# Row matrices of the lead-in sort split over POOL, ScalarE and VectorE

## The chip, the cores and the metric

The kernel runs on one core of one Trainium2 chip. The metric is the device time of one execution in microseconds (us). For the kernel before, three runs gave 8667.58, 8670.53 and 8680.19 us; the median is 8670.53 us.

## What is computed

A graph has N = 10000 nodes and E = 640000 edges. Every edge takes the 64 x 4 features of its source node, multiplies them with a 4 x 4 matrix made of the edge's Y and the tensor cg, scales each channel with a radial weight, and adds the result to its target node. At the end the 64 channels are mixed:

```python
R = _silu(edge_feat @ w_rad)                              # (E, C)
xs = x[src]                                               # (E, C, M)
tp = jnp.einsum('eci,ef,ifo->eco', xs, Y, cg)             # (E, C, M)
msg = R[:, :, None] * tp
agg = _segment_sum(msg.reshape(-1, C * M), dst, N).reshape(N, C, M)
return jnp.einsum('ncm,cd->ndm', agg, w_mix)
```

## The kernel before

The segment sum needs the edges of a target node together, so the kernel sorts the edges' payloads (9 words: a key of target and source, four of Y, four of edge_feat) by target in two passes. The first pass (`pass1`) sorts into 18 groups of 576 nodes, the second (`pass2`) each group into buckets of 32 nodes; `messages` then gathers the source rows and does the arithmetic bucket by bucket. The edges are cut into three parts (`SPLIT`, 30%, 35.5%, 34.5%). Pass 1 of the first part runs alone at the start: this is the **lead-in**, 1488 tiles of 128 edges. Everything later (pass 1 of the other parts, pass 2, the messages) is interleaved by `groups`, which starts when the lead-in's groups lie in DRAM: its first load, `Wt` (L760), reads what the lead-in has stored.

A pass takes its tiles in chunks, twelve tiles each in pass 1, so the lead-in has 124 chunks (0 to 123). `route` moves a chunk with one matmul per tile: the payloads, spread over 14 slots of a row (`spread`: the mask L569 and `X` L572, VectorE), are multiplied by a 128 x 128 matrix that is one where the row of the edge equals the column. These **row matrices** `oh` come from `rows`. Of a chunk's twelve, VectorE makes the first six with one comparison (L588; its constant 0..127, `v128`, is in PSUM), and ScalarE the last six with a Square each (L594: (row - i)^2) and one Relu of 1 - 2x over all six (L595). TensorE accumulates the twelve products in PSUM (L602; each float32 product is two MATMUL records in the trace), ScalarE copies the result to `rt` (L609), and POOL stores its 128 rows to the DRAM tensor `grp` with one indirect DMA (L613). The positions come from small matmuls (L532, L534), ScalarE (L542) and VectorE (L551 to L561), the payload words from L714 to L716, and every 20 chunks or so a table is worked out (`digits`, `tables`).

`oh` and `X` have three buffers each, `rt` has 38 in the lead-in.

What sets the order. In the lead-in the order on SP is the order in which the code issues; for the other engines a planner lays down one list per engine beforehand, from its own estimates of when each instruction can start, earlier code first where several can. On the chip each engine goes through its list. In the code a chunk's store comes eight chunks behind its row matrices (`self.ls`). SP's list holds the loads of the edges (`ys`, `es`, `da`, `si`) and, woven between them, the zeroing of what later stages write: first the buckets (`bkt<-z`, L248), then the groups of parts 1 and 2 (`grp<-z`, L230, 36 DMAs of about half a MB). The latter go to the tensor `grp`, which the indirect stores of the lead-in also may write anywhere, so a clear waits for the stores that precede it in the code, and the stores that follow wait for the clear. In the list planned for the kernel before, the store of chunk 102, the first one behind the last clear, stands behind the row matrices of chunk 108.

In the rest of the kernel PE, VectorE and ScalarE follow an order written out by `groups`.

Of the kernel before, what the change touches and what calls it, by code (L numbers as in the profile page):

```python
# [21 lines left out]
OP = mybir.AluOpType  # L22
# [3 lines left out]
P = 128  # L26
# [30 lines left out]
def weave(main, side, ratio):  # L57

    acc = 0.0
    for said in main:  # L60
        acc += ratio
        while acc >= 1.0:
            acc -= 1.0
            next(side, None)
        yield said
    yield from side


def run(gen):
    for _ in gen:  # L70
        pass


class Kernel:
# [276 lines left out]
    def tables(self, ps, D, nt, rows, kov, base, cap):  # L351
# [157 lines left out]
        self.tab[ps.key] = (sb, idx, N, tg if ps.carry else None)  # L509
        yield  # L510

    def route(self, ps, quad, nt, table):


# [2 lines left out]
        nc, wk, tc, T, Q = self.nc, self.ph, self.tc, ps.T, 2  # L517
# [60 lines left out]
        def rows(c):  # L578

            row, _ = MS[c // (2 * Q)]  # L580
            o = c % (2 * Q) * T
            m = min(T, nt - c * T)
            (_, _, _, tg), i = table(c)
            on = ps.carry and i > 0
            oh = self.ph.tile([P, 12, P], F, name="oh", bufs=3)
            v = max(m - ps.act, 0)
            if v:
                nc.vector.tensor_tensor(oh[:, :v, :], self.v128.unsqueeze(1).to_broadcast([P, v, P]),  # L588
                                        row[:, o:o + v].unsqueeze(2).to_broadcast([P, v, P]), op=OP.is_equal)

            at = [row[:, o + u:o + u + 1] for u in range(v, m)] + ([tg[:, i - 1:i]] if on else [])
            sq = self.ph.tile([P, 7, P], F, name="sq")
            for u, to in enumerate(at):
                nc.scalar.activation(sq[:, u, :], self.i128, AF.Square, bias=to, scale=-1.0)  # L594
            nc.scalar.activation(oh[:, v:v + len(at), :], sq[:, :len(at), :], AF.Relu, bias=self.ones[:, 0:1], scale=-2.0)  # L595
            XO[c] = (XO[c], oh, m, on)
# [26 lines left out]
        for k in range(-3 * Q, N + self.ls):  # L623
            if 0 <= k - lag - 1 < N:
                evict(k - lag - 1)
            if 0 <= k - lag < N:
                move(k - lag)
            if k % 2 and 0 <= k + 5 < N:

                while self.pos:  # L630
                    yield "held"
                self.pos = ps.key
                places((k + 5) // 2)
            if k % 2 == 0 and 0 <= k + 4 < N:
                placed((k + 4) // 2)
                self.pos = None
            if k % 2 == 0 and 0 <= k + 6 < N:
                prepare((k + 6) // 2)
            if 0 <= k < N:
                spread(k)  # L640
                yield "half"
                rows(k)
            if k % 2 and 0 <= k + 3 < N:
                slots((k + 3) // 2)
            if 0 <= k - self.ls < N:
                store(k - self.ls)

            yield (HEAVY - 2 if k < N else HEAVY) if 0 <= k < N + lag else 1

    def pass1(self, part, first):  # L650
# [73 lines left out]
        while True:  # L724

            if side is None and j + 1 < nb and (j < 1 or k >= cut[j]):
                j += 1
                side = front(j)
            need = of[min(max(k + 6, 0), nch - 1)] not in TB
            if side is not None and (need or acc >= 1.0 or self.held == ps.key):  # L730
                acc -= 1.0
                said = next(side, "end")
                if said == "end":
                    side = None
                    continue
                yield said
                if need or said != "held":
                    continue
                acc = 0.0
            said = next(route, "end")  # L740
            if said == "end":
                break
            if said == "half":
                yield 2
                continue
            if said != "held":
                k = k + 1
                acc = min(acc + 2.0, 8.0)
            yield said
# [289 lines left out]
    def groups(self):  # L1039
# [26 lines left out]
        for v in range(4 * u):  # L1066
# [24 lines left out]
            next(main)  # L1091
        assert not later
        run(main)
        run(sort)

    def chunks(self, part):
# [109 lines left out]
    def run(self):  # L1206
        tile_pool, nc = self.tc.tile_pool, self.nc
        order = [self.NG - 1] + list(range(self.NG - 1))
        self.segs = [(k, g) for k in range(len(SPLIT)) for g in order]
        with tile_pool(name="p1", bufs=2) as self.ph:  # L1210
            self.rt_bufs, self.ls = 38, 8
            self.lag, self.ahead, self.early = 2, 3, 1
            self.z = self.ph.tile([P, 2048], F, name="z", bufs=1)
            nc.gpsimd.memset(self.z, 0.0)
            self.consts()

            with self.tc.manual_schedule(engines={mybir.EngineType.SP}):
                first = self.pass1(0, 8)
                next(first)
                run(self.clear_groups(0, nc.scalar))  # L1220
                for _ in range(40):
                    next(first, None)
                while self.held:
                    next(first)
                self.weights()
                later = itertools.chain(self.clear_buckets(),
                                        *(self.clear_groups(k, nc.sync) for k in range(1, len(SPLIT))))
                run(weave(first, later, 0.185))
                self.sorted = 1
        with tile_pool(name="p2", bufs=2) as self.ph:  # L1230
            self.rt_bufs, self.ls = 5, 4
            self.lag, self.ahead, self.early = 1, 2, 0
            self.p1.NC = 14
            with self.tc.manual_schedule(engines={mybir.EngineType.PE, mybir.EngineType.DVE,
                                                  mybir.EngineType.Activation}):
                self.groups()
        with tile_pool(name="p3", bufs=1) as self.ph:
            self.overflow_consts()
            self.overflow(self.p1, self.kov[:, 0:1])
            self.overflow(self.p2, self.kov[:, 1:2])  # L1240
# [29 lines left out]
```

## Time and profile before

| | us |
|---|---|
| median of 3 runs | 8670.53 |
| time of the profiled execution, as its span | 8660.7 |
| what the median has beyond that span | 9.8 |
| last store of the lead-in starts (L613) | 523.22 |
| first load of the next stage issues (L760) | 525.91 |

Times inside a profile count from the start of its span. A row of the timeline gives start, duration, engine, line, operation and tiles, how many were merged, and in brackets the engine's idle time before it with what seems to have ended it. A row of the windows view gives, for a stretch, its length and then for each engine the busy time and in parentheses the number of instructions; the last three columns are TensorE's granted clock, the busy share of the DMA engines and the GB/s. The lines view gives busy time, mean ns of one instruction, and the idle time before. "SPq" is the issue of a DMA on SP's queue.

### The profile page before, as it was taken

What the parts mean: (1) busy time and instruction counts of PE and PEld (TensorE: products, weight loads), DVE (VectorE), ACT (ScalarE), POOL (GpSimd) and SP (SyncE); (2) the same over time, 40 slices, a digit from 0 to 9 for tenths busy, and PEclk for the clock granted to TensorE, in tenths of its full rate; (3) what the DMA queues carried; (4) which work ended last, traced back from release to release, by engine and by line L of the source; (5) the groups of instructions that cost most, each with busy time, mean ns of one, the idle gap of its engine ahead of it and who ended that gap; (6) DMA issues with size and microseconds to landing.
All of it is one profiled execution on the core that took longest, in us unless ns stands there. A gap on an engine that the chain in (4) does not pass through costs nothing. (4 is left out here: it accounts for less than half of the span.)

```text
span 8660.7 us, 149335 instructions
## 1 busy us (share of the span) xinstructions
PE 6942.9 (80%) x52148; PEld 6380.0 (74%) x52148; DVE 7173.7 (83%) x13741; ACT 4089.0 (47%) x11736; POOL 6041.3 (70%) x6308
## 2 busy tenths in 40 slices
PE   7978888888888778888888888866888878788875
PEld 6867777777777677777777777766777767777764
DVE  8989899889998788999989998877877768677754
ACT  6866555555556455454544554433333323333310
POOL 1236777667777767777777777777777777777775
PEclk9989999889999889999889899888998889888887
DMA  9313434334433434444444444444444444444442
GB/s 169 104 58 99 123 115 119 103 113 117 121 110 111 122 106 132 135 132 138 133 130 136 135 133 134 128 138 132 128 125 125 125 124 124 122 128 125 124 123 83
DMA packets 696289, 1056.64 MB, mean 122 GB/s; under 512 B 252018, under 2 KB 500226, under 8 KB 695536
## 3 DMA queue, kind: packets, MB, share of 16 engines
q0 software_dynamic: 286560, 746.71, 30.3%
q1 hardware_dynamic: 406384, 292.76, 12.2%
q8 instruction: 412, 6.75, 0.3%
q10 hardware_dynamic: 2592, 7.63, 0.3%
q14 instruction: 341, 2.79, 0.1%
HBM read 856.08 MB, written 207.12 MB: 123 GB/s over the span
## 5 line engine op out<-in xcount | busy, mean ns | idle before, releaser
L893 POOL DMA_INDIRECT xg<-in_x_dram,sidx x5321 | 5067.8, 952 | 1739.3 <-issue 1386.5
L602 PE MATMUL pr<-X,oh 128*128 128x126 f32 (+1 forms) x21112 | 2765.2, 289 | 395.7 <-ACT rt L609 215.6
L958 PE MATMUL G<-S,xg 128*128 128x128 f32 x21284 | 2953.1, 302 | 98.1 <-DVE Gp L987 62.8
L602 PEld LDWEIGHTS pr<-X,oh 128*128 128x128 f32 x21112 | 2638.2, 201 | 477.8 <-ACT rt L609 264.2
L958 PEld LDWEIGHTS G<-S,xg 128*128 128x128 f32 x21284 | 2803.5, 215 | 139.3 <-DVE Gp L987 86.2
L945 DVE TENSOR_TENSOR xg<-xg,pre 128x1536 f32<-128x1536 f32 (+1 forms) x939 | 1556.8, 1658 | 710.5 <-DMA xg<-in_x_dram,sidx 586.4
L594 ACT ACTIVATE sq<-i,rowf 128x128 f32<-128x128 f32 x5605 | 1735.7, 393 | 13.9 <-DVE rowf L559 13.4
L572 DVE TENSOR_TENSOR X<-dv,Wt 128x1512 f32<-128x1512 f32 (+4 forms) x958 | 1588.4, 1658 | 149.0 <-PE pr L602 94.8
L927 ACT ACTIVATE pre<-pre 128x384 f32<-128x384 f32 (+1 forms) x939 | 430.8, 459 | 1694.7 <-PE pre L924 1204.7
L595 ACT ACTIVATE oh<-sq,ones 128x768 f32<-128x768 f32 (+3 forms) x958 | 932.1, 973 | 32.9 <-issue 5.5
L938 DVE TENSOR_TENSOR S<-dv,pay 128x768 f32<-128x768 f32 (+1 forms) x939 | 857.4, 913 | 48.0 <-PE G L958 2.8
L613 POOL DMA_INDIRECT grp<-rt,idx x417 | 415.5, 996 | 585.9 <-ACT rt L609 240.1
L588 DVE TENSOR_TENSOR oh<-dv,rowf 128x640 f32<-128x640 f32 (+2 forms) x922 | 792.2, 864 | 0.5
L613 POOL DMA_INDIRECT bkt<-rt,idx x541 | 543.2, 1004 | 221.7 <-issue 125.8
L911 PE MATMUL pre<-identb,e 128*108 128x128 bf16 x1878 | 277.3, 231 | 523.4 <-DVE xg L945 513.6
L911 PEld LDWEIGHTS <-e 128*108 128x108 bf16 x1878 | 219.9, 133 | 604.5 <-issue 515.2
L916 ACT ACTIVATE sT<-pre 108x256 bf16<-108x256 f32 x939 | 353.5, 376 | 631.1 <-PE pre L911 628.4
L1006 PE MATMUL po<-wf,Gs 128*128 128x256 f32 (+2 forms) x1392 | 382.3, 436 | 150.7 <-DVE Gs L987 150.5
L542 ACT ACTIVATE pc<-pp 128x432 f32<-128x432 f32 (+3 forms) x506 | 243.7, 482 | 524.1 <-DVE pos L551 407.3
L1006 PEld LDWEIGHTS po<-wf,Gs 128*128 128x128 f32 (+2 forms) x1392 | 277.5, 205 | 238.3 <-DVE Gs L987 166.8
L609 ACT ACTIVATE rt<-pr 128x135 f32<-128x135 f32 (+1 forms) x958 | 258.8, 273 | 269.4 <-DMA bkt<-rt,idx 181.4
L923 PE MATMUL pre<-wr,sT 108*128 108x192 bf16 x939 | 240.2, 256 | 142.2 <-ACT sT L916 141.8
(240 smaller groups left out, 5309.3 us busy)
## 6 DMA issues: line engine op xcount, KB each, us to landing
xg<-in_x_dram,sidx POOLq DMA_INDIRECT x5321
sums<-Gp SPq DMA_DIRECT2D x626, 128.0 KB
old<-sums SPq DMA_DIRECT2D x626, 128.0 KB
bkt<-z SPq DMA_DIRECT2D x24, 994.5 KB
pay<-bkt SPq DMA_DIRECT2D x34, 486.0 KB
ys<-in_Y_dram SPq DMA_DIRECT2D x104, 96.0 KB
es<-in_edge_feat_dram SPq DMA_DIRECT2D x104, 96.0 KB
out_dram<-ot SPq DMA_DIRECT2D x69, 128.0 KB
```

Source lines behind the costliest of these rows:

```text
L572: nc.vector.tensor_tensor(X[:, :m, :].rearrange("p t (s w) -> p t s w", w=W), msk.unsqueeze(3).to_broadcast([P, m, ps.r, W]), QD[c // Q][1 ...
L588: nc.vector.tensor_tensor(oh[:, :v, :], self.v128.unsqueeze(1).to_broadcast([P, v, P]), row[:, o:o + v].unsqueeze(2).to_broadcast([P, v, P ...
L594: nc.scalar.activation(sq[:, u, :], self.i128, AF.Square, bias=to, scale=-1.0)
L595: nc.scalar.activation(oh[:, v:v + len(at), :], sq[:, :len(at), :], AF.Relu, bias=self.ones[:, 0:1], scale=-2.0)
L602: nc.tensor.matmul(pr[:, :ps.rw], oh[:, u, :], X[:, u, :], start=(u == 0), stop=(not on and u == m - 1))
L613: st = nc.gpsimd.indirect_dma_start(out=ps.dst, out_offset=bass.IndirectOffsetOnAxis(ap=idx[:, i:i + 1], axis=0), in_=RT.pop(c), in_offset ...
L893: nc.gpsimd.indirect_dma_start(out=xg[:, t, :], out_offset=None, in_=self.x, in_offset=bass.IndirectOffsetOnAxis(ap=si[:, u:u + 1], axis=0))
L911: nc.tensor.matmul(pre[:KR, 256 + 128 * h:384 + 128 * h], e[:, 36 * t:36 * t + KR], self.identb, start=True, stop=True)
L938: nc.vector.tensor_tensor(S[:, :ut], self.eq[:, :ut].unsqueeze(3).to_broadcast([P, ut, NB, 4]), pb[:, :, 1:5].unsqueeze(2).to_broadcast([P ...
L945: nc.vector.tensor_tensor(V, V, R.unsqueeze(3).to_broadcast([P, ut, 64, 4]), op=OP.mult)
L958: nc.tensor.matmul(G[:, h].rearrange("p n f -> p (n f)"), V[:, t, 32 * h:32 * h + 32, :].rearrange("p c i -> p (c i)"), S[:, t].rearrange( ...
L1006: nc.tensor.matmul(po[:nn, :256], Gs[:, h, f].rearrange("p b n -> p (b n)")[:, :nn], self.wf[:, h, f, :], start=(h + f == 0), stop=(h + f ...
```

## The change

In the lead-in the comparison for the first five tiles of a chunk moves to POOL, one `tensor_scalar` per tile, against the same constant in SBUF (`i128`) with the tile's row numbers as a per-partition scalar. VectorE keeps two tiles (the sixth and seventh), ScalarE the last five. `self.aid` is 5 in the lead-in and 0 in the rest, where the split stays as it was.

```diff
+    def act(self, ps):
+        return 5 if self.aid else ps.act
...
-            v = max(m - ps.act, 0)
-            if v:
-                nc.vector.tensor_tensor(oh[:, :v, :], self.v128.unsqueeze(1).to_broadcast([P, v, P]),
-                                        row[:, o:o + v].unsqueeze(2).to_broadcast([P, v, P]), op=OP.is_equal)
+            v = max(m - self.act(ps), 0)
+            g = min(self.aid, v)
+            for u in range(g):
+                nc.gpsimd.tensor_scalar(oh[:, u, :], self.i128, row[:, o + u:o + u + 1], None, op0=OP.is_equal)
+            if g < v:
+                nc.vector.tensor_tensor(oh[:, g:v, :], self.v128.unsqueeze(1).to_broadcast([P, v - g, P]),
+                                        row[:, o + g:o + v].unsqueeze(2).to_broadcast([P, v - g, P]), op=OP.is_equal)
...
             self.lag, self.ahead, self.early = 2, 3, 1
+            self.aid = 5
...
             self.lag, self.ahead, self.early = 1, 2, 0
+            self.aid = 0
```

## The prediction

> **What bounds the kernel now.** The change touches only the lead-in, so the first question is where the lead-in ends and what ends it. I read the windows view first (columns PE, PEld, DVE, ACT, POOL, then clock, DMA share, GB/s), in the stretches that the rest of the argument uses.
>
> ```profile
> span 8660.7 us, 149335 instructions
> 40.00:240.00 200.00, 168.57 (x1256) 148.05 (x1255) 176.50 (x367) 151.07 (x457) 37.46 (x38) 0.92 0.92 154
> 240.00:496.00 256.00, 239.36 (x1900) 212.51 (x1900) 251.83 (x465) 229.09 (x691) 62.37 (x64) 0.99 0.28 95
> 496.00:521.00 25.00, 23.63 (x195) 22.16 (x194) 20.92 (x23) 16.06 (x46) 18.81 (x20) 1.00 0.15 45
> ```
>
> From 240 to 496 us VectorE is busy 251.83 of 256 us, TensorE 239.36, ScalarE 229.09, POOL 62.37. Seen like this, moving work from VectorE to the idle POOL looks free. The timeline says otherwise. These are POOL's and SP's rows at four places, and the first of the next stage:
>
> ```profile
> 214.25 0.97 POOL L613 DMA_INDIRECT grp<-rt,idx  x1 [1.77 <-ACT rt L609]
> 240.32 0.97 POOL L613 DMA_INDIRECT grp<-rt,idx  x1 [25.09 <-ACT pc L542]
> ...
> 288.12 0.97 POOL L613 DMA_INDIRECT grp<-rt,idx  x1 [0.30 <-ACT Wt L715]
> 290.45 0.34 SPq L230 DMA_DIRECT2D grp<-z  x1
> 295.07 0.97 POOL L613 DMA_INDIRECT grp<-rt,idx  x1 [5.98 <-ACT Wt L715]
> 296.35 0.97 POOL L613 DMA_INDIRECT grp<-rt,idx  x1 [0.30 <-ACT sq L594]
> ...
> 496.41 0.97 POOL L613 DMA_INDIRECT grp<-rt,idx  x1 [4.30 <-ACT oh L595]
> ...
> 523.22 0.97 POOL L613 DMA_INDIRECT grp<-rt,idx  x1 [0.30 <-issue]
> 525.91 0.34 SPq L760 DMA_DIRECT2D Wt<-grp  x1
> 526.02 0.18 DVE L770 TENSOR_SCALAR base<-bb 128x18 f32<-128x18 f32 x1 [8.17 <-DMA grp<-rt,idx]
> ```
>
> The next stage starts when the last store has landed (525.91, and VectorE has then idled 8.17 us). From 240 us on the stores do not follow the compute; they alternate with the clears of `grp` on SP: a store (288.12) lands, the next clear issues (290.45), it lands, and the next stores go (295.07, 296.35). POOL stands idle some 6 us for each clear, and the brackets name engines that have nothing to do with it. How many clears, stores and row matrices there are:
>
> ```profile
> L230 SPq DMA_DIRECT2D grp<-z x36: 332/343/1655, 234.0 to 493.4; - x36
> L613 POOL DMA_INDIRECT grp<-rt,idx x124: 969/971/1315, 44.1 to 523.2; - x124
> 0.00:240.00 240.00, 37.46 (x38) 0.94 0.90 168
> 240.00:496.00 256.00, 62.37 (x64) 0.99 0.28 95
> 496.00:525.00 29.00, 21.39 (x22) 0.98 0.15 46
> 0.00:240.00 240.00, 43.47 (x46) 0.94 0.90 168
> 240.00:496.00 256.00, 66.80 (x71) 0.99 0.28 95
> ```
>
> The third to fifth rows are the windows of L613, the last two those of L588. Between 240 and 496 us 36 clears and 64 stores make 256 us, or 7.1 us a clear and 4.0 us a store. Meanwhile 71 chunks got their row matrices, one per 3.6 us. So the stores fall behind: the 38 + 64 = 102 stores done at 496 us stand against 46 + 71 = 117 chunks whose VectorE half has begun, a lead of 15. The 22 stores that are left then go in one run, 1.275 us apart (26.81 us from 496.41 to 523.22), and only just catch up with the last chunk. **Two limits meet at 524 us**: the compute, and the chain of clears and stores. Relief for VectorE shifts only the first.
>
> **The change, part by part.** Rows for the durations:
>
> ```profile
> L572 DVE TENSOR_TENSOR X<-dv,Wt 128x1512 f32<-128x1512 f32 x73 | 126.0, 1727 | 1.9
> L588 DVE TENSOR_TENSOR oh<-dv,rowf 128x768 f32<-128x768 f32 x72 | 68.1, 945 | 0.0
> L588 DVE TENSOR_TENSOR oh<-dv,rowf x922: 275/818/958, 37.8 to 8265.1; 128x640 f32<-128x640 f32 x100, 128x768 f32<-128x768 f32 x82, 128x128 f32<-128x128 f32 x3
> L594 ACT ACTIVATE sq<-i,rowf 128x128 f32<-128x128 f32 x434 | 135.8, 398 | 2.8 <-DVE rowf L559 2.5
> 499.55 2.92 PE L602 MATMUL pr<-X,oh 128*128 128x126 f32 x24 [0.16 <-DVE oh L588]
> 502.62 2.91 PE L602 MATMUL pr<-X,oh 128*128 128x126 f32 x24 [0.16 <-DVE oh L588]
> L149 POOL IOTA i<- 128x128 f32 x1 | 0.2, 236 | 0.0
> L267 POOL IOTA prm<- 128x128 f32 x1 | 0.4, 438 | 0.0
> L1214 POOL MEMSET z<- 128x2048 f32 x1 | 1.8, 1804 | 0.3 <-POOLq L1258 0.3
> ```
>
> *VectorE.* Six tiles take 945 ns, one takes 275, so a tile is (945 - 275) / 5 = 134 ns and two tiles 0.41 us: 0.54 us less per chunk. *ScalarE* loses one Square of six, 135.8 / 434 = 0.31 us of its time, and a sixth of a Relu. Neither of the two can shorten a chunk much below the present pace: undisturbed, a chunk takes 502.62 - 499.55 = 3.07 us, and TensorE's own 24 records take 2.91 of it. Even without any other limit the pace gains 0.16 us of 3.07, or 5%.
>
> *Up to 240 us.* The DMA engines are 92% busy here, TensorE 168.57 of 200 us. VectorE idles 23.5 us and would lose 40 x 0.54 = 22 us of work, so the bounds of an earlier first clear are 0 and 22 us. I take **-5 us**, near the lower end, as SP's list reaches that clear only behind the bucket zeroing, and that is DMA time.
>
> *POOL's new work.* No POOL comparison is in this trace. The nearest rows of the same 128 x 128 size are the two iotas, 0.236 and 0.438 us, which only write; the memset makes 0.88 ns an element, 0.11 us for 128. One `tensor_scalar` also reads, so I take 0.30 us, with 0.20 and 0.44 as ends: **1.5 us per chunk** (1.0 to 2.2). By itself that fits beside a store of 1.275 us: 2.8 us of a chunk's 3.6.
>
> *What is queued behind a blocked store.* The five comparisons of a later chunk now stand in POOL's list between stores. A store that waits for a clear holds up every comparison behind it, then the matmuls of that chunk, and with three `oh` buffers soon VectorE and ScalarE. The free lead of 15 chunks is gone; what is left is the lead of the planned list, where store 102 stands behind the row matrices of chunk 108. I assume that the new list keeps about that, with one chunk more as POOL is otherwise free. Then at the last clear 14 chunks' comparisons are still to be made, where the trace has 7 left. POOL must from 496.41 on do 22 stores and 14 groups of five: 22 x 1.275 + 14 x 1.5 = 49.1 us, so the last store ends at 545.5 instead of 524.2: **+21 us** (TensorE needs 14 x 2.91 = 41 us beside it, which does not decide). With 1.0 and 2.2 us a group it is +14 and +31 us.
>
> [...]
>
> *The chain between 240 and 496 us.* 63 groups of comparisons (45 to 108) must run in it, 94 us by my price. POOL's idle time there is 256 - 62.37 = 194 us, so they can lie under the waits for clears. Those that the list puts between a clear's landing and the next stores lengthen that round instead. Ends: none, and all 94 us. POOL is in its run of stores about a quarter of the time (62.37 of 256 us), so I take a fifth: **+19 us**.
>
> [...]
>
> *The sum:* -5 + 21 + 19 = +35 us. Everything behind L760 runs as before, with `self.aid` 0 and its order written out, so the shift goes through to the end: span 8660.7 + 35 = 8695.7, and with the 9.8 us that the median has beyond the span, **8705.5 us**. The cover on which the change lives is POOL's idle time; it is idle because it waits, and that is the time in which it can't do anything else either.
>
> **The rivals.** About 0.2% (17 us) is what a measurement of this kernel can tell from no change.
>
> *The comparisons get past the stores* (the new list runs them far ahead, or POOL is not held). For it: the planner knows of the clears, and a faster compute in its estimate would widen the lead. Against it: three `oh` buffers. Then compute gains up to 5%, but the 36 clears at 7.1 us and 22 stores end where they did, less what the first clear comes earlier: 0 to -22 us, 8648 to 8670.5. Most of that lies within 17 us, since the DMA engines hold the first clear.
>
> *POOL becomes the bound.* At 0.44 us a comparison, a chunk's store and group take 1.275 + 2.2 = 3.5 us, as long as a chunk now. If besides every group falls into a round of the chain, the price is 63 x 2.2 + 31 = 170 us, 8840 us. It decides from about 0.35 us a comparison, or where the list puts the comparisons behind the landing. Half of that, +85 us, is where I part it from the forecast.
>
> *The split doesn't reach the clock at all*: list and lead stay and the tail is hidden: 8670 us, part of "same".
>
> **How the numbers follow.** Forecast (+17 to +85 us): 0.60. POOL as the bound (above +85): 0.15. No coupling, within 17 us: 0.16. No coupling and an early first clear, below -17: 0.09. So slower 0.75, within 0.2% 0.16, faster 0.09. The range goes from -10 us (8660), inside the case without coupling, to +100 us (8770), a little into POOL as the bound; about 0.1 lies beyond each end.
>
> **What would show it.** Right: the new profile has POOL rows of L588's place between the stores, of some 0.3 us each; waits of TensorE for POOL's `oh` from 240 us on; a lead of some 8 chunks instead of 15 where the last clear lands; the last store near 545 to 560 us and L760 behind it by 2.7 us; the rest of the span as long as before. Wrong: clears that still issue 7.1 us apart with compute running ahead of the stores as before (then the coupling fails), a last store before 520 us, a comparison far from 0.3 us, or a change behind L760.

## The result and the profile after

The changed kernel takes 8732.41 us (median of 5 runs, 8727.85 to 8734.75) against 8675.29 us for the kernel before beside it: a ratio of 1.0067, 95% interval 1.0056 to 1.0078, or 57 us slower. Forecast were 35 us, with a range that reaches to 100. The profiled execution has a span of 8730.1 us, 69.4 more than before. That is more than the 57 us because the profiled execution of the kernel before (span 8660.7 us) was quicker than all five of its runs here (8667.58 us and more), while the changed kernel's median lies 2.3 us beyond its span. The runs were taken in batches, each with the kernel before beside it, and in one batch everything behind the lead-in took longer (10586.37 us for the kernel before), so that of this batch only ratios and lead-in ends count.

The same four places of POOL's and SP's timeline, in the changed kernel (the store is now L619, the comparison L592, the next stage's load L766). First the stores around 245 us, where the clears of `grp` begin, then the first store behind the last clear, then the **run-out** (the 22 stores behind the last clear) and its end:

```profile
245.56 1.25 POOL L619 DMA_INDIRECT grp<-rt,idx  x1 [0.17 <-issue]
247.11 0.97 POOL L619 DMA_INDIRECT grp<-rt,idx  x1 [0.30 <-PE pp L537]
248.11 2.94 POOL L592 TENSOR_SCALAR oh<-i,rowf 128x128 f32<-128x128 f32 x5
255.06 1.05 POOL L619 DMA_INDIRECT grp<-rt,idx  x1 [4.02 <-PE pp L537]
...
533.88 1.05 POOL L619 DMA_INDIRECT grp<-rt,idx  x1 [0.17 <-issue]
...
550.98 2.93 POOL L592 TENSOR_SCALAR oh<-i,rowf 128x128 f32<-128x128 f32 x5
554.09 1.05 POOL L619 DMA_INDIRECT grp<-rt,idx  x1 [0.17 <-ACT sq L600]
555.19 2.93 POOL L592 TENSOR_SCALAR oh<-i,rowf 128x128 f32<-128x128 f32 x5
...
595.82 0.97 POOL L619 DMA_INDIRECT grp<-rt,idx  x1 [0.30 <-issue]
598.55 0.34 SPq L766 DMA_DIRECT2D Wt<-grp  x1
```

Five comparisons take 2.93 us, 0.59 us each, where 0.30 was put in. Towards the end POOL does nothing but five comparisons and one store, over and over, 4.2 us a chunk (550.98 to 555.19), without a pause. Split at the same stores as before, the lead-in became longer like this:

| | before | after | difference |
|---|---|---|---|
| store 38 starts | 240.32 | 245.56 | +5.2 |
| store 38 to store 102 (the chain with the clears) | 256.1 | 288.3 | +32.2 |
| store 102 to store 123 (the run-out) | 26.8 | 61.9 | +35.1 |
| last store to the next stage's load | 2.7 | 2.7 | 0.0 |
| everything behind that load, to the end of the span | 8134.8 | 8131.6 | -3.2 |

The whole loss is in the lead-in, as forecast; 72.6 us there, and what follows is as long as it was. How the loss splits between the chain and the run-out depends on the profile of the kernel before that one compares with (last experiment); their sum changes by 7 us. The windows of the changed kernel (columns PE, PEld, DVE, ACT, POOL, clock, DMA share, GB/s):

```profile
40.00:240.00 200.00, 174.99 (x1237) 150.99 (x1237) 159.86 (x365) 131.03 (x402) 175.30 (x261) 0.91 0.98 149
240.00:530.00 290.00, 257.27 (x1768) 218.35 (x1766) 218.39 (x444) 192.45 (x583) 255.81 (x388) 0.94 0.25 87
530.00:597.00 67.00, 55.42 (x341) 45.54 (x340) 30.80 (x46) 30.73 (x88) 61.35 (x89) 0.92 0.07 23
```

POOL, idle for 194 of 256 us before, is now the busiest engine after TensorE (255.81 against 257.27 of 290 us), and VectorE has room: 218 of 290 us. That relief is real and buys nothing. Who waits for whom between 240 and 597 us says why (engine, line, who for, us in total, times, longest):

```profile
ACT rt L615 <- PE pr L608: 100.2, 54, 6.4
PEld pr L608 <- POOL oh L592: 64.3, 136, 3.4
DVE pos L554 <- ACT pc L545: 48.6, 22, 6.4
PE pr L608 <- POOL oh L592: 26.4, 19, 3.1
```

TensorE waits for POOL's row matrices, ScalarE for TensorE, VectorE for ScalarE.

### The profile page after: what moved, and what is told of

It reads as the page before. It is cut to its first block, busy times and chain, and to the rows that moved or that the text cites. A ratio compares the mean times of both kernels' runs of the same rounds, so it can differ in the third digit from the quotient of the medians.

```text
span 8730.1 us, 150147 instructions
## 1 busy us (share of the span) xinstructions
PE 6964.3 (80%) x52148; PEld 6381.6 (73%) x52148; DVE 7132.9 (82%) x13741; ACT 4049.3 (46%) x11612; POOL 6420.2 (74%) x6928
## 5 line engine op out<-in xcount | busy, mean ns | idle before, releaser
L608 PE MATMUL pr<-X,oh 128*128 128x126 f32 (+1 forms) x21112 | 2811.8, 291 | 421.9 <-ACT rt L615 218.4
L600 ACT ACTIVATE sq<-i,rowf 128x128 f32<-128x128 f32 x5481 | 1700.7, 392 | 19.1 <-DVE rowf L562 19.1
L601 ACT ACTIVATE oh<-sq,ones 128x896 f32<-128x896 f32 (+4 forms) x958 | 918.4, 959 | 37.9 <-issue 5.5
L594 DVE TENSOR_TENSOR oh<-dv,rowf 128x640 f32<-128x640 f32 (+3 forms) x922 | 726.6, 793 | 0.5
L619 POOL DMA_INDIRECT bkt<-rt,idx x541 | 543.1, 1004 | 222.8 <-issue 122.2
L619 POOL DMA_INDIRECT grp<-rt,idx x417 | 421.4, 1010 | 240.8 <-issue 82.8
L592 POOL TENSOR_SCALAR oh<-i,rowf 128x128 f32<-128x128 f32 x620 | 370.5, 611 | 47.8 <-DVE rowf L562 36.3
```

Of the source, the lines that this page charges most:

```text
L594: nc.vector.tensor_tensor(oh[:, g:v, :], self.v128.unsqueeze(1).to_broadcast([P, v - g, P]), row[:, o + g:o + v].unsqueeze(2).to_broadcast ...
L608: nc.tensor.matmul(pr[:, :ps.rw], oh[:, u, :], X[:, u, :], start=(u == 0), stop=(not on and u == m - 1))
L619: st = nc.gpsimd.indirect_dma_start(out=ps.dst, out_offset=bass.IndirectOffsetOnAxis(ap=idx[:, i:i + 1], axis=0), in_=RT.pop(c), in_offset ...
```

## The experiments

Two causes were open. **Queue coupling**: the comparisons stand in POOL's list behind stores that wait for clears, and hold up the compute. **POOL's pace**: 2.94 us of comparisons and 1.26 us of store make 4.2 us a chunk, more than the 3.6 us that a chunk took. The edits below are to the changed kernel or to the one before. "Lead-in end" is the start of the next stage's load in that run's profile; the kernel before has 525.91 and, in a second profile (last experiment), 528.08 us. Where no other value is given, "later" and "earlier" mean against these two.

### One tile on POOL, clears left in place

```diff
-        return 5 if self.aid else ps.act
+        return 6 if self.aid else ps.act
-            self.aid = 5
+            self.aid = 1
```

> POOL makes one tile's row matrix per chunk instead of five (VectorE five, ScalarE six); the clears of grp stay between the stores. If only POOL's working time counts (a comparison measured at 0.59 us, a store 1.275): 1.87 us of a chunk's 3.07, so nothing is lost, -2 to +3 us against before. If a comparison behind a store that waits for a clear holds the compute (queue coupling): in the planned list the store behind the last clear stands behind 111 chunks' comparisons, so 13 chunks are left to compute there instead of 7; 13 x 3.07 plus some 4 us from 497 us on ends at 541 instead of 524, with the rounds of the chain hardly longer: +10 to +20 us.

Measured: 8680.83 us against 8653.27, ratio 1.0032 (1.0019 to 1.0044), 28 us slower; lead-in end 542.75, some 16 us later. The +10 to +20 us expected of queue coupling fit the lead-in's end; the median lies above them. POOL is busy 96 of the 240 us below, and still TensorE waits for it. The lines view from 240 to 480 us:

```profile
L608 PE MATMUL pr<-X,oh 128*128 128x126 f32 x1410 | 184.7, 289 | 32.5 <-POOL oh L592 28.3 <-DVE X L575 2.5 <-DVE oh L594 1.1
L619 POOL DMA_INDIRECT grp<-rt,idx x59 | 59.9, 1016 | 116.8 <-DMA grp<-z 66.8 <-ACT oh L601 13.2 <-ACT sq L600 6.3
L592 POOL TENSOR_SCALAR oh<-i,rowf 128x128 f32<-128x128 f32 x59 | 36.4, 626 | 27.4 <-PE pr L608 11.4 <-ACT sq L600 7.2 <-DVE dv L572 2.8
```

POOL idles 66.8 us for clears in front of stores, and TensorE 28.3 us for POOL's matrices, which POOL makes in 36.4 us. The run-out shows the lost lead: store 102 starts at 489.67, and the last one comes only at 540.04, as the compute has 13 chunks to do by then:

```profile
489.67 1.05 POOL L619 DMA_INDIRECT grp<-rt,idx  x1 [3.41 <-DMA grp<-z]
...
534.15 0.97 POOL L619 DMA_INDIRECT grp<-rt,idx  x1 [1.52 <-ACT rt L615]
537.09 0.96 POOL L619 DMA_INDIRECT grp<-rt,idx  x1 [1.97 <-ACT rt L615]
540.04 0.96 POOL L619 DMA_INDIRECT grp<-rt,idx  x1 [1.98 <-ACT rt L615]
```

At the end POOL waits for `rt`, not the reverse. The coupling is shown, without POOL being short of time.

### Two tiles on POOL, clears left in place

```diff
-            self.aid = 5
+            self.aid = 2
```

(and 6 for ScalarE, as above)

> Two tiles on POOL, VectorE four, ScalarE six, clears left between the stores. POOL's own time is twice that of the one-tile kernel (2.44 us a chunk), still below TensorE's 2.91. In the planned list the first store behind the last clear stands behind 111 chunks' comparisons, as with one tile. Queue coupling expects the loss of the one-tile kernel again, whatever the number of tiles: +15 to +35 us. If POOL's working time makes the loss, it doubles: +45 us and more.

Measured: 8676.26 against 8655.05 us, ratio 1.0027 (1.0016 to 1.0037), 21 us slower; lead-in end 539.44. Twice the comparisons cost no more than one, net of VectorE's relief, which is twice as large here; if POOL's working time made the loss, the expectation was that it doubles. The table further down sets the two apart.

### The clears freed

Clears of parts 1 and 2 and stores of part 0 touch different rows of `grp`, but both name the whole tensor, so they were ordered. This edit tells the planner that they need not be:

```diff
+                c = eng.dma_start(v[:, o:o + m], self.z[:, :m])
+                if k:
+                    if self.in_group["grp"]:
+                        self.tc.declare_no_dep(c.ins, group="grp", reason="part 0 writes none of these rows")
+                    self.tc.add_to_no_dep_group("clr", c.ins)
+                    self.cleared += 1
...
+            if self.cleared and not self.sorted:
+                tc.declare_no_dep(st.ins, group="clr", reason="part 0 writes none of these rows")
```

In the changed kernel, with five tiles on POOL:

> The changed kernel, but the clears of the groups of parts 1 and 2 and the stores of part 0, which write different rows, no longer wait for each other. If POOL's working time is the bound: 124 chunks x 4.2 us from some 47 us on end at about 570 us instead of 597, so +40 to +50 us against before remain. If the rounds of clears and stores were the main cost: the end is back near 524 us, within 10 us of before.

Measured: 8716.93 against 8653.27 us, ratio 1.0071 (1.0057 to 1.0084); lead-in end 574.56, 24 us earlier than with the clears in place and some 47 later than before. The +40 to +50 us expected of POOL's working time fit the lead-in's end; the median (+64 us) lies above them. POOL is busy 312 of the 330 us from 240 to 570; its timeline in the middle of that:

```profile
400.37 2.94 POOL L597 TENSOR_SCALAR oh<-i,rowf 128x128 f32<-128x128 f32 x5
403.47 1.05 POOL L624 DMA_INDIRECT grp<-rt,idx  x1 [0.17 <-issue]
404.57 2.94 POOL L597 TENSOR_SCALAR oh<-i,rowf 128x128 f32<-128x128 f32 x5
407.68 1.05 POOL L624 DMA_INDIRECT grp<-rt,idx  x1 [0.17 <-ACT rt L620]
```

4.2 us a chunk, with no wait for a clear: POOL's pace alone makes most of the changed kernel's loss.

In the kernel before:

> The kernel before, with the clears and the lead-in's stores freed of each other in the same way. If two limits met at 524 us, as the prediction has it: the stores now follow the compute at once, but the compute still ends at about 521 us, so 0 to -3 us. If the chain of clears was the only bound: the end moves by 10 us and more.

Measured: 8652.82 against 8653.27 us, ratio 0.9998 (0.9989 to 1.0007). Stores now follow the compute at once (store 102 at 448.31 us instead of 496.41), and nothing is won in the time. The last result leaves for `rt` 274.7 us after chunk 45's; in the kernel before that is 274.4. Two limits did meet. The lead-in end in this profile, 517.10, is earlier than before's, for the most part already at chunk 45 (239.24 against 246.52); the second profile of the kernel before also has 241.68 there, so the median decides.

With one tile on POOL, and with two:

> One tile per chunk on POOL, VectorE five, ScalarE six, and the clears freed of the lead-in's stores. If what one POOL tile cost in the run with the clears (28 us) was the compute held behind stores that waited for clears, the loss goes and VectorE's relief of 0.13 us a chunk shows: -4 to -14 us against before. If a POOL comparison costs the compute something by itself, 10 us and more of the loss stay.

> Two tiles on POOL, VectorE four, ScalarE six, clears freed. POOL then has 1.18 + 1.26 = 2.44 us of work a chunk, below TensorE's 2.91, so queue coupling by the clears expects a gain, -8 to -20 us against before (VectorE 0.27 us a chunk, bounded by TensorE's 0.16 where the clock is full). If POOL's time is in the way even below the chunk's pace, 0 to +15 us.

Measured in the batch with 10586.37 us for the kernel before: one tile 10566.67 us, ratio 0.9974 (0.9964 to 0.9983), lead-in end 511.35; two tiles 10553.65 us, ratio 0.9964 (0.9951 to 0.9977), lead-in end 499.89. What one and two tiles lost with the clears in place, they now win, and more than the 4 to 14 and 8 to 20 us that were expected. With one tile, TensorE's wait for POOL is gone from the row that showed 28.3 us of it (lines view, 240 to 480 us):

```profile
L613 PE MATMUL pr<-X,oh 128*128 128x126 f32 x1637 | 205.1, 279 | 8.6 <-DVE oh L599 3.6 <-DVE X L580 2.5 <-DVE dest L481 0.9
```

> Two tiles on POOL with the clears freed, once more, as the earlier runs were on a chip on which everything behind the lead-in was slower. Lead-in end again near 500 us, -20 to -35 us against before.

Measured: 8635.82 against 8655.05 us, ratio 0.9979 (0.9970 to 0.9988), lead-in end 499.51. This version beats both kernels, the one before by 19 us, at the edge of the 20 to 35 that were expected. Its windows row for 240 to 480 us, and POOL's timeline in it:

```profile
240.00:480.00 240.00, 233.25 (x1872) 211.60 (x1871) 233.20 (x453) 225.20 (x681) 158.16 (x211) 1.00 0.29 101
```

```profile
401.14 1.20 POOL L597 TENSOR_SCALAR oh<-i,rowf 128x128 f32<-128x128 f32 x2 [0.33 <-issue]
403.42 1.05 POOL L624 DMA_INDIRECT grp<-rt,idx  x1 [1.07 <-DVE rowf L567]
405.37 1.24 POOL L597 TENSOR_SCALAR oh<-i,rowf 128x128 f32<-128x128 f32 x2 [0.90 <-issue]
```

TensorE, VectorE and ScalarE are all at 94 to 97%, POOL at 66% with short pauses: now it takes work without being in anyone's way.

> Three tiles on POOL, VectorE four, ScalarE five, clears freed. POOL then has 1.77 + 1.26 = 3.03 us a chunk, just above TensorE's 2.91, ScalarE 0.4 us less than with two. If POOL's time per chunk is the bound once it passes TensorE's: as good as two tiles within 8 us, not better. If ScalarE's six tiles hold the two-tile kernel: 5 us and more better than it.

Measured: 8639.78 against 8655.05 us, ratio 0.9983 (0.9974 to 0.9992), lead-in end 497.92. As good as two tiles, as expected, but not for the reason in the expectation. Its windows row:

```profile
240.00:480.00 240.00, 229.11 (x1868) 208.40 (x1867) 234.51 (x446) 204.19 (x611) 199.81 (x280) 1.00 0.28 98
```

POOL is busy 83%, and TensorE's MATMULs wait for it for 2.7 us in all, so POOL's time is not the bound here. VectorE, which makes four tiles in both kernels, is busy 98 and 97%; that it sets the pace of both is likely, and no run shows it.

Set side by side, the lead-in's end by tiles on POOL:

| tiles on POOL | on VectorE, ScalarE | clears between the stores | clears freed |
|---|---|---|---|
| 0 | 6, 6 | 525.9, 528.1 | 517.1 |
| 1 | 5, 6 | 542.8 | 511.4 |
| 2 | 4, 6 | 539.4 | 499.9, 499.5 |
| 3 | 4, 5 | not run | 497.9 |
| 5 | 2, 5 | 598.6 | 574.6 |

Along a row only the clears' order differs, and the lists planned with it: the coupling costs 31 us with one tile, 40 with two and 24 with five. Down a column VectorE's relief and POOL's load change together; the 15 us that one and two tiles lose against none are what is left of the coupling after that relief.

### The work on POOL without its use

The kernel before, and beside it five comparisons a chunk into a tile that nobody reads:

```diff
+            for u in range(5 if self.aid else 0):
+                du = self.ph.tile([P, P], F, name="du", bufs=2)
+                nc.gpsimd.tensor_scalar(du, self.i128, row[:, o + u:o + u + 1], None, op0=OP.is_equal)
```

> The kernel before, with five POOL comparisons per chunk beside it whose results nobody reads. VectorE and ScalarE keep all their work, and no matmul waits for POOL. If POOL's working time is what the change costs (1.26 + 2.95 = 4.2 us a chunk against 3.6): the stores are as late as in the changed kernel, +55 to +70 us. If the cost is that matmuls wait for POOL's matrices: the compute ends at 521 us as before and only the stores behind it are late, +20 to +40 us.

Measured: 8787.71 against 8653.27 us, ratio 1.0150 (1.0136 to 1.0163), lead-in end 649.30. Both expectations missed, and the assumption under them was wrong: the compute does wait for POOL here, though not for its results. The waits from 240 to 490 us:

```profile
DVE rowf L559 <- POOL du L593: 47.0, 6, 17.8
PE pr L605 <- DVE oh L588: 41.1, 9, 17.9
PEld pr L605 <- DVE oh L588: 39.6, 12, 18.2
POOL grp L616 <- DMA grp<-z: 36.2, 7, 7.2
```

VectorE may not overwrite the row numbers (`rowf`, two buffers) before POOL has read them, and waits 47.0 us for that. No `oh` buffer meters these comparisons, so POOL runs them in lumps, and stores wait behind the lumps (here 35 comparisons, seven chunks' worth, in one go):

```profile
422.45 1.05 POOL L616 DMA_INDIRECT grp<-rt,idx  x1 [3.15 <-ACT sq L597]
423.81 0.97 POOL L616 DMA_INDIRECT grp<-rt,idx  x1 [0.30 <-ACT oh L598]
424.81 20.50 POOL L593 TENSOR_SCALAR du<-i,rowf 128x128 f32<-128x128 f32 x35
```

So this run separates nothing; it shows that here the busy reader, POOL, held up the writer, VectorE, as well.

### The other part of the change alone

```diff
-            g = min(self.aid, v)
+            g = 0
```

(ScalarE five tiles, VectorE seven, POOL none)

> One part of the change alone: ScalarE makes five tiles in the lead-in, VectorE seven, POOL none. If VectorE sets the pace of the compute (0.13 us more a chunk over some 100 chunks) and the compute is one of two limits that meet: +8 to +14 us. If the pace is TensorE's or ScalarE's: -3 to +3 us.

Measured (in the batch with 10586.37 us for before): 10597.78 us, ratio 1.0014 (1.0005 to 1.0023), lead-in end 539.50, 11 us later than the 528.08 of the same batch, as expected if VectorE sets the pace. One tile more on VectorE is 0.13 us a chunk: VectorE did set the pace of the compute, and ScalarE's relief does not make up for it.

### What a POOL instruction costs

```diff
+                for n in (32, 128, 512):
+                    du = self.ph.tile([P, 512], F, name="du", bufs=2)
+                    if c % 4 == 0:
+                        nc.gpsimd.tensor_scalar(du[:, :n], self.z[:, :n], row[:, o + u:o + u + 1], None, op0=OP.is_equal)
+                    elif c % 4 == 1:
+                        nc.gpsimd.tensor_scalar(du[:, :n], self.z[:, :n], 3.0, None, op0=OP.is_equal)
+                    elif c % 4 == 2:
+                        nc.gpsimd.tensor_scalar(du[:, :n], self.z[:, :n], 3.0, None, op0=OP.add)
+                    else:
+                        nc.gpsimd.tensor_copy(du[:, :n], self.z[:, :n])
```

> The kernel before, with three POOL instructions per chunk beside it whose results nobody reads: 32, 128 and 512 elements each, by turns (chunk number modulo 4) a comparison with a per-partition scalar, a comparison with a constant, an addition of a constant, a copy. If 0.59 us for 128 elements is mostly a price per instruction: the 32-element comparison takes 0.5 us or more and the 512-element one below 1.2 us. If it is a price per element: 0.15 to 0.25 us and 2 us or more. If the scalar operand or the comparison is what is slow: the addition or the copy is cheaper by half at 128 elements.

Measured (one execution, by form; the number behind the comma is the mean in ns):

```profile
L595 POOL TENSOR_SCALAR du<-z,rowf 128x512 f32<-128x512 f32 x31 | 48.6, 1567 | 0.0
L597 POOL TENSOR_SCALAR du<-z 128x512 f32<-128x512 f32 x31 | 45.9, 1482 | 0.0
L599 POOL TENSOR_SCALAR du<-z 128x512 f32<-128x512 f32 x31 | 45.9, 1481 | 0.0
L601 POOL COPY du<-z 128x512 f32<-128x512 f32 x31 | 20.2, 652 | 0.0
L595 POOL TENSOR_SCALAR du<-z,rowf 128x128 f32<-128x128 f32 x31 | 18.9, 611 | 0.0
L599 POOL TENSOR_SCALAR du<-z 128x128 f32<-128x128 f32 x31 | 16.4, 530 | 0.0
L597 POOL TENSOR_SCALAR du<-z 128x32 f32<-128x32 f32 x31 | 9.0, 290 | 0.1
L601 POOL COPY du<-z 128x128 f32<-128x128 f32 x31 | 9.1, 293 | 0.0
```

From 128 to 512 elements a comparison with a scalar operand grows by 956 ns, 2.5 ns an element, with some 0.29 us beside it; a copy by 359 ns, 0.93 ns an element. Comparison and addition with a constant cost the same (1482 and 1481 ns at 512 elements), the scalar operand some 85 ns (1567 against 1482). So neither of the first two readings fits alone: at 128 elements about half is per instruction and half per element. Per element it is the comparison and the addition that are slow, not the reading: the copy, which reads as much, takes 652 ns at 512 elements.

### The kernel before, once more

> The kernel before once more, for a second profile of it: how far the stretch up to 240 us, the lead-in's end (525.9 us) and the rest (8134.8 us) differ between two executions of one program. Both theories expect the stretch from 240 us to the lead-in's end within 3 us of the first profile.

Measured: the first clear at 229.54 instead of 234.04 us, the lead-in end 528.08 instead of 525.91, in the batch with the longer rest (span 10581.2 us). Not as expected: from the last result of chunk 45 to the next stage it is 286.4 instead of 279.4 us, and parts of it differ more. Store 38 to store 102 takes 247.9 instead of 256.1 us, the run-out 41.9 instead of 26.8, as here the last stores wait for the compute:

```profile
525.44 0.97 POOL L613 DMA_INDIRECT grp<-rt,idx  x1 [1.83 <-ACT rt L609]
```

In the first profile the stores catch up only with the last chunk, here some ten chunks sooner, which fits two limits that meet. So single profiles of one program differ by some 7 us from chunk 45 to the lead-in's end and by up to 15 us in a part of it. Against this second profile the changed kernel's chain is 40.4 us longer instead of 32.2 and its run-out 20.0 instead of 35.1; the two together are 60.5 instead of 67.3. In the table of lead-in ends, differences of 7 us carry nothing.

In the batches with 8653 and 8655 us no profile of the kernel before was taken. There the medians of seven kernels lie 8 to 16 us further from before's median than their lead-in ends lie from the mean of its two profiles (one tile with clears: +28 against +16), which points to a kernel before that is some 11 us quicker there than in these profiles. In which stretch stays open.

## Why the prediction was right, and where its sizes were off

**The signs it named.** TensorE's waits for POOL came, the 2.7 us from the last store to the next stage, and the unchanged rest. Where the last clear lands, 112 chunks' comparisons had begun and 102 stores were done, a lead of 10 chunks where some 8 were named. Two signs came out against it: a comparison took twice 0.3 us, and the last store started at 595.82 us, not between 545 and 560.

**What bounds.** Right: the lead-in's end is set by POOL's last store, two limits met at 524 us (the freed kernel before gains nothing), and relief for VectorE alone can move only one of them.

**Up to 240 us, -5.** Measured +5.2 at store 38, and +9.9 against the second profile, where it starts at 235.68. A gain did not come: POOL is busy 175 of the 200 us up to 240, which leaves it hardly any room at 4.2 us a chunk. With one and two tiles and the clears in place store 38 starts at 229.78 and 226.51, so the gain is there when POOL has time.

**POOL's price, 0.30 us a comparison with 0.20 and 0.44 as ends.** This is the step that was mis-sized. It is 0.59 to 0.61 us, outside both ends. The nearest rows were chosen by size, and all of them only write; a copy of that size, with a read as well, took 0.293 us, just what was put in, but the comparison and the addition grew by 2.5 ns an element from 128 to 512. "That fits beside a store: 2.8 us of a chunk's 3.6" was therefore wrong; it is 4.2.

**The run-out, +21.** Measured +35.1, or +20.0 against the second profile of the kernel before, whose own run-out is longer; that the second figure agrees with the forecast is luck, as the price in it was half. Its structure held: the list behaves as assumed, only that it left 12 chunks instead of 14 for the time behind store 102. 22 stores x 1.275 + 12 x 2.95 = 63.5 us, measured 62.9 (533.88 to 596.79).

**The chain, +19.** Measured +32.2 (+40.4 against the second profile), of 64 x 2.95 = 189 us of comparisons: 17 to 21% fell into the rounds, where a fifth was taken. The share was right, the price was not.

**The sum.** The same sum with 2.95 us a group, 14 groups and a fifth gives -5 + 42 + 37 = +74 us; the profile has +72.6 at the lead-in's end. That the two are so near is in part luck: against the first profile the terms are off by +10, -7 and -5, which cancel. The median moved by 57. The 9.8 us that the prediction added beyond the span were mostly not a fixed part of an execution's time, as one execution has 1.9 beyond its own span (8731.98 against 8730.1 in the changed kernel); the rest is the distance of the profiled execution from the median of others.

**The first rival** was told as if no coupling meant no loss. The freed changed kernel refutes that: 574.56 us. **POOL as the bound** was the rival, with its point of decision at 0.35 us a comparison, and that point was passed. The changed kernel is the forecast and this rival at once: the coupling, less what VectorE's relief gains, costs some 15 us of lead-in (one and two tiles), POOL's pace alone some 47, both together 72. Only the rival's price of 170 us was far off, since it let every group fall into a round; about four fifths lay under waits. The line at +85 us between the two cases was drawn by that price, so that the forecast's number came out in its own case though half the mechanism belongs to the other.

**What stands behind a blocked store.** The +21 and the +19 rest on this: a store that waits for a clear holds up the comparisons behind it in POOL's list. That was the author's assumption, and the run with a single comparison a chunk bears it out: POOL idles 66.8 us in front of stores that wait for clears, TensorE 28.3 us for POOL, and with the clears freed TensorE's wait for POOL is gone from its row (lead-in end 542.75 to 511.35).

## What to carry to other kernels

POOL was idle because it waited in its own queue, and that time was not free: with one comparison a chunk it idled 66.8 us for clears and TensorE 28.3 us for it. So first look at what stands ahead of the new work in that queue, and at what lead the queue's waits have let the others build up. Here the wait itself was needless, and with it gone the same idea, in a smaller dose (two tiles, 2.4 us of POOL a chunk), turned from 21 us lost into 19 us won. Price an operation from a row that does the same kind of work, not only the same number of elements: 0.30 us was put in from rows that only write, and 0.59 us was measured.

## What the runs showed of the hardware that was not expected

VectorE's small copies were longer beside POOL's comparisons. The same two lines of VectorE before (240 to 500 us) and after (240 to 530 us):

```profile
L716 DVE COPY Wt<-si 128x24 int32<-128x24 int32 x36 | 6.8, 190 | 0.0
L572 DVE TENSOR_TENSOR X<-dv,Wt 128x1512 f32<-128x1512 f32 x73 | 126.0, 1727 | 1.9
```

```profile
L722 DVE COPY Wt<-si 128x24 int32<-128x24 int32 x34 | 12.6, 369 | 0.0
L575 DVE TENSOR_TENSOR X<-dv,Wt 128x1512 f32<-128x1512 f32 x67 | 115.6, 1726 | 10.2 <-PE pr L608 7.9 <-DVE dv L572 0.5
```

The copy from SBUF to SBUF takes 369 ns instead of 190; the large product, one operand of which is in PSUM, takes 1726 as before. From 60 us to these stretches' ends, the changed kernel's copies take 366 ns in the mean where one of POOL's comparisons runs at the same time (48 copies) and 186 where only a store does (6); in the kernel before, the copies beside no work of POOL take 177 (45). Beside a store alone the figures differ: 214 in the kernel before (12) and 270 in the freed changed kernel (14). With two tiles and the clears freed all these copies take 224 in the mean (240 to 480 us). What in the hardware makes the copies longer is not shown. VectorE has time for them in the changed kernel, where it is busy 218 of 290 us.

TensorE's granted clock was 0.94 in the changed kernel's stretch from 240 to 530 us, in which it waits for POOL, 0.99 in the kernel before's (240 to 500) and 1.00 in that with two tiles and freed clears (240 to 480). TensorE's own records are longer there as well: 298 ns a MATMUL (lines view, 240 to 530 us), against 279 and 280. The other kernels in which TensorE waits for POOL's matrices go the same way: 0.95 and 289 ns with one tile, 0.94 and 292 with two (240 to 480), 0.96 and 295 with five and the clears freed (240 to 570). That the waits are the cause is not shown.

```profile
L608 PE MATMUL pr<-X,oh 128*128 128x126 f32 x1572 | 231.1, 298 | 31.8 <-POOL oh L592 21.4 <-DVE X L575 3.0 <-DVE row L560 1.2
```
